# Three GpSimd multiplications moved behind a group of loads, and one output piece moved ahead of a tile's scores

## The chip, the core and the metric

The kernel runs on one core of a Trainium2 chip. The metric is the device time of one execution in microseconds (us), and the time given for the kernel before is the median of three runs.

## What is computed

A retention layer (an attention whose weights decay with distance) is followed by a feed-forward layer with a snake activation. Cut to what matters, the reference is:

```python
# q, k, v: 4 batches x 8 heads x 768 positions x 64
for t in range(768):
    state = gamma * state + outer(k[t], v[t])      # per batch and head
    y[t] = q[t] @ state / 8                        # 64 -> 1/sqrt(64)
x = y with heads side by side                      # 3072 tokens x 512
h = x @ w_in                                       # 512 -> 2048
g = h + sin(alpha * h)**2 / (alpha + 1e-9)
out = g @ w_out                                    # 2048 -> 512, float32
```

## The kernel before

**Tiles and groups.** The 768 positions of a batch are cut into 6 chunks of 128, so there are 24 tiles of 128 tokens by 512. `order` (P in the code) lists them: P[0] to P[3], also called e0 to e3, are the first chunks of the four batches, which need no state; then come chunks 1 to 5 of batch 0 (P[4] to P[8]), and so on. The sixth tile is P[5]. The tiles make groups: the first has four tiles, each of the other ten has two.

**One tile.** `stage_T` turns q and k on TensorE and copies them out of PSUM (DVE, line 279). `stage_A` makes the scores (PE, line 293) and multiplies them with the decay or the mask into `aT` (DVE, line 302). `stage_M` multiplies the state (line 332) and the scores (line 336) into the PSUM tile `py`, adds the tile to the state (line 312), and multiplies `py` with the decay table `qg[:, c]` of the tile's chunk into `xT` (DVE, line 343); then `keep_S` copies the state out (ScalarE, ACT in the profile, line 319). For a later chunk the next state needs v scaled by position: `scale_v` multiplies v in place by `kg` (line 155). `decay_table(c, engine)` makes `qg[:, c]` from `qg[:, 0]` (line 223).

**The feed-forward layer.** A `Slot(g, f)` is 128 hidden units of a group: 4 matmuls with w_in into a PSUM tile `ph` (line 567), the sine on ACT (line 570), the square on ACT (line 575) or on DVE (line 577, chosen with `sq("D")`), and the add on DVE (line 582), which reads the sine's square from SBUF and `ph` from PSUM, writes `gT` and frees `ph`. An output piece is one matmul of 128x512 with w_out (line 592); `F(ts, lo, hi)` issues pieces lo to hi-1 of token tile ts of the first group. The PSUM tiles with tag "mm" share four banks in turn; "ty", "pa" and "ps" are one bank each.

**The order of the work.** It is written out by hand, and each engine does its own instructions in the order of the program. For the first group that is lines 754 to 896, with the slots named w[0] to w[15], and w[20] and w[21] for the fourth tile's columns (four units each, 128 wide). In the order of the "mm" tiles there, w[7], w[6], w[3], w[5] are followed by w[20], w[21], w[11], w[9], and these by w[8], w[10], w[13], w[12].

**GpSimd's queue.** GpSimd (POOL in the profile) issues all loads of q, k, v and the weights, in the order of the program, and they go through one queue (q0). Lines 157 to 161 issue v of e0; q, k and v of e1 and of e2; w_in(0) and w_in(1) (quarters): nine loads. Lines 689 to 691 then run the three multiplications of the change, and lines 692 to 701 issue q, k, v of e3, the other six quarters of w_in and w_out, and q, k, v of P[4], P[5] and P[6]. Counted from the first, v of P[4] is the 21st load and q of P[5] the 22nd. Behind these stand more loads mixed with scalings of v (lines 779 to 810).

Of the kernel before, what the change touches and what calls it, by code (L numbers as in the profile page):

```python
# [15 lines left out]
def kernel(  # L16
# [15 lines left out]
    nc = tc.nc  # L32
# [36 lines left out]
    def chunk_of(t, j):  # L69
        b, c = divmod(j, NCH)  # L70
        return t[b, :, c * C:(c + 1) * C, :].rearrange("h s d -> s h d")

    def paired(j):

        return j in order[1:B]

    def pairs_of(t, j):
        b, c = divmod(j, NCH)
        return t[b, :, c * C:(c + 1) * C, :].rearrange("h (i f) d -> i h (f d)", f=2)

    def load_chunk(j, names="qkv"):
        for name, src in (("q", q), ("k", k), ("v", v)):
            if name not in names:
                continue
            if name == "v":
                t = big.tile([128, H, D], BF16, name="vr", tag="vr", bufs=10)
            elif name == "q" and paired(j):
                if "pairs" not in raw:
                    raw["pairs"] = work.tile([64, B, H, 2, D], BF16, name="qp", tag="gT", bufs=2)
                t = raw["pairs"][:, order.index(j)]  # L90
                nc.gpsimd.dma_start(out=t.rearrange("i h f d -> i h (f d)"), in_=pairs_of(src, j))
                raw[name, j] = t
                continue
            else:
                if ("qk", j) not in raw:
                    raw["qk", j] = big.tile([128, 2, H, D], BF16, name="qkr", tag="qkr", bufs=9)
                t = raw["qk", j][:, "qk".index(name)]
            nc.gpsimd.dma_start(out=t, in_=chunk_of(src, j))  # L98
            raw[name, j] = t
# [3 lines left out]
    def wide(j):  # L103
        return j >= NCH + 2 and j % NCH > 0
# [28 lines left out]
    def load_w_out(i):  # L133
        nc.gpsimd.dma_start(out=w_out[:, i * fo:(i + 1) * fo, :], in_=w_out_v[:, i * fo:(i + 1) * fo, :])
# [16 lines left out]
    def scale_v(j, eng):  # L151
        t, by = raw["v", j], kg
        if wide(j):
            t, by = t.rearrange("i f p d -> i (f p) d"), kgq
        eng.tensor_mul(t, t, by[:, j % NCH, :, None].to_broadcast([128, H, D]))  # L155
# [66 lines left out]
    def decay_table(c, eng):  # L222
        eng.tensor_mul(qg[:, c], qg[:, 0], step[:, c, :, None].to_broadcast([128, NP, C]))
# [43 lines left out]
    def stage_T(j, eng=None, tag="ty"):  # L267
        st["qkT", j] = work.tile([128, 2 * NP, 128], BF16, name="qkT", tag="qkT", bufs=6)
        copy = nc.scalar.copy if eng is nc.scalar else nc.vector.tensor_copy
        if paired(j):  # L270
            for i, t in enumerate((tag, "pa")):
                pt = psum.tile([128, NP, 128], BF16, name="pt", tag=t)
                turn_half(j, i, pt)
                leave_T(j, i, pt, copy)
            return
        pt = psum.tile([128, 2 * NP, 128], BF16, name="pt", tag=tag, bufs=4 if tag == "mm" else 1)
        for i in range(2):
            turn_half(j, i, pt[:, i * NP:(i + 1) * NP, :])
        copy(st["qkT", j], pt)
# [7 lines left out]
    def stage_A(j, parts=1):  # L287
        qkT = st["qkT", j]
        pa = psum.tile([128, 2, NP, 128], F32, name="pa", tag="pa")
        for p in range(NP):  # L290
            for e in range(2):
                r = slice(64 * e, 64 * e + 64)
                nc.tensor.matmul(pa[:, e, p, :], qkT[r, NP + p, :], qkT[r, p, :],  # L293
                                 start=(p == 0), stop=True, skip_group_check=True)
        aT = work.tile([128, 2, NP, 128], BF16, name="aT", tag="aT", bufs=2)
        flat = "p e n t -> p (e n) t"
        if parts > 1:
            for h in range(0, NP, NP // parts):
                r = slice(h, h + NP // parts)
                nc.vector.tensor_mul(aT[:, :, r], pa[:, :, r], dec[:, :, r])  # L300
        else:
            nc.vector.tensor_mul(aT.rearrange(flat), pa.rearrange(flat), dec.rearrange(flat) if j % NCH == 0 else mask_bc)  # L302
        st["aT", j] = aT
# [17 lines left out]
    def stage_M(j, tag="ty"):  # L321
        c = j % NCH
        g, i = place[j]
        if g not in xT:
            xT[g] = work.tile([128, KS, sizes[g] * C], BF16, name="xT", tag="xT", bufs=3)
        qkT, aT, vs = st["qkT", j], st["aT", j], raw["v", j]
        py = psum.tile([128, NP, 128], F32, name="py", tag=tag)
        if c > 0:
            for p in range(NP):
                for e in range(2):  # L330
                    r = slice(64 * e, 64 * e + 64)
                    nc.tensor.matmul(py[r, p, :], s_bd[c % 2][:, p, r], qkT[:, p, :],  # L332
                                     start=(p == 0), stop=True, skip_group_check=True)
        for p in range(NP):
            for e in range(2):
                nc.tensor.matmul(py[64 * e:64 * e + 64, p, :], vs[:, 2 * p + e, :], aT[:, e, p, :],  # L336
                                 start=(c == 0 and p == 0), stop=True, skip_group_check=True)
        x = xT[g][:, :, i * C:(i + 1) * C]
        if c == 0:
            nc.scalar.copy(x, py)  # L340
            return
        ps = stage_S(j) if c < NCH - 1 else None
        nc.vector.tensor_mul(x, py, qg[:, c])
        if ps is not None:
            if wide(j + 1):
                swapped(s_b[(c + 1) % 2][0], ps, nc.scalar.copy)
                swapped(s_f[0], ps, nc.vector.tensor_copy)
            else:
                keep_S(j, ps)
# [239 lines left out]
    def ff_out(g, ts, f):  # L589
        if (g, ts) not in po:  # L590
            po[g, ts] = psum.tile([128, d_model], F32, name="po", tag="mm", bufs=4)
        nc.tensor.matmul(po[g, ts], gT[g][:, f, ts * C:(ts + 1) * C], w_out[:, f, :],  # L592
                         start=(f == 0), stop=(f == FF - 1))
        if f == FF - 1:
            take(g, ts)
# [49 lines left out]
    e0, e1, e2, e3 = P[:B]  # L645
# [40 lines left out]
    nc.vector.reciprocal(rec_alpha, rec_alpha)  # L686
    decay_table(1, nc.vector)

    scale_v(e0, nc.gpsimd)
    decay_table(2, nc.gpsimd)  # L690
    decay_table(3, nc.gpsimd)
    load_chunk(e3)
    load_w_out(0)
    load_w_in(2)
# [2 lines left out]
    load_w_out(2)  # L697
    load_w_out(3)
    load_chunk(P[4])
    load_chunk(P[5])  # L700
    load_chunk(P[6])

# [44 lines left out]
    def F(ts, lo, hi):  # L747
        for f in range(lo, hi):
            ff_out(0, ts, f)
# [136 lines left out]
    SK(e0)()  # L886
    F(2, 6, 7)
    stage_T(P[5], nc.vector, "mm")
    F(2, 7, 10)
    scale_v(P[5], nc.vector)  # L890
    stage_A(P[5])
    F(2, 10, 11)
    stage_M(P[4])
    F(2, 11, 15)
    stage_M(P[5])
# [68 lines left out]
```

## Time and profile before

| what | value |
|---|---|
| median of three runs | 211.04 us (210.78 to 211.46) |
| the profiled execution | 210.3 us |
| its span, first to last instruction | 208.4 us |
| granted TensorE clock | 1.000 |
| PE busy | 202.9 us, 97% of the span |
| DVE, ACT busy | 158.7 and 159.5 us |
| GpSimd busy | 109.5 us, of which most stands before 125 us |
| the loads of q, k, v and weights (q0) | 13.38 MB in 75968 packets |

The profile comes from one execution; the times in it count from the start of its span. PE is TensorE, PEld its weight loads, DVE VectorE, ACT ScalarE, POOL GpSimd, SP the engine that issues the stores. A row of a timeline gives the start, the time from the first start to the last end, the engine, the line, the operation, the output and inputs, and how many instructions are merged; a bracket gives the idle time before the row and what ended it. The ends of matmuls are modelled, so rows of PE overlap a little.

### The profile page before, as it was taken

How to read it: one execution, taken by the hardware profiler on the slowest of the kernel's cores; microseconds unless marked ns; L12 is line 12 of the kernel's file. 1: busy time of each engine (PE TensorE's matmuls, PEld its weight loads, DVE VectorE, ACT ScalarE, POOL GpSimd, SP SyncE). 2: the span in 40 equal slices, each digit the busy share in tenths (PEclk: the TensorE clock that was granted, in tenths of full speed). 3: DMA queues.
4: the chain of work that ended last, by engine and by line, in shares of the span. 5: the costliest groups of instructions: out<-in, count | busy, mean ns of one | idle time of the engine just before them, and what ended most of it. 6: DMA issues, size and time to landing. Idle time of an engine off the chain costs nothing.

```text
span 208.4 us, 5987 instructions
## 1 busy us (share of the span) xinstructions
PE 202.9 (97%) x2427; PEld 132.3 (63%) x2427; DVE 158.7 (76%) x363; ACT 159.5 (77%) x344; POOL 109.5 (53%) x148
## 2 busy tenths in 40 slices
PE   6998999999999999999999999999999999999994
PEld 2654644567776667666666666666766766666653
DVE  7867897876988597787788778779878778686540
ACT  7858798548997878888888888886787787888821
POOL 8899333898979979999999330000413101000000
PEclk9999999999999999999999999999999999999999
DMA  8999999999999999999999903412415110110112
GB/s 128 156 199 179 201 207 179 155 211 183 132 115 96 193 178 162 170 139 176 174 142 174 173 36 68 101 46 58 104 53 55 53 50 3 53 50 0 50 53 101
DMA packets 98747, 24.78 MB, mean 119 GB/s; under 512 B 91280, under 2 KB 95776, under 8 KB 98720
## 3 DMA queue, kind: packets, MB, share of 16 engines
q0 software_dynamic: 75968, 13.38, 85.6%
q1 hardware_dynamic: 22608, 10.96, 25.0%
q8 instruction: 19, 0.31, 0.6%
q10 hardware_dynamic: 144, 0.07, 0.1%
q14 instruction: 8, 0.07, 0.1%
HBM read 27.27 MB, written 6.29 MB: 161 GB/s over the span
## 4 chain that ended last, share of the span: by engine, by line
PE 94%; DVE 3%; ACT 1%; issue 0%; DVEq 0%
PE ph L567 39%; PE po L592 39%; PE spare L637 3%; PE pa L293 2%; PE poh L617 2%; PE py L397 2%; PE pt L249 1%; PE py L336 1%; PE py L510 1%; PE py L332 1%; PE pa L413 1%; PE pa L433 1%; DVE gT L582 1%; PE ps L312 1%; DVE qkT L265 0%
## 5 line engine op out<-in xcount | busy, mean ns | idle before, releaser
L582 DVE SCALAR_TENSOR_TENSOR gT<-s,rec_alpha,ph 128x256 bf16<-128x256 f32 (+3 forms) x184 | 82.1, 489 | 26.6 <-ACT s L575 25.7
L570 ACT ACTIVATE s<-ph,alpha_sb 128x256 f32<-128x256 f32 (+3 forms) x184 | 79.1, 480 | 29.4 <-PE ph L567 28.3
L567 PE MATMUL ph<-xT,w_in 128*128 128x256 bf16 (+3 forms) x736 | 98.6, 277 | 0.0
L592 PE MATMUL po<-w_out,gT 128*128 128x512 bf16 x368 | 95.3, 380 | 0.0
L567 PEld LDWEIGHTS <-w_in 128*128 128x128 bf16 x736 | 70.5, 98 | 30.4 <-issue 0.4
L575 ACT ACTIVATE s<-s 128x512 f32<-128x512 f32 (+1 forms) x91 | 56.4, 623 | 2.7
L592 PEld LDWEIGHTS <-gT 128*128 128x128 bf16 x368 | 33.9, 98 | 25.9 <-DVE gT L582 0.3
L438 POOL CAST s_b<-s_f 128x256 bf16<-128x256 f32 x10 | 4.0, 399 | 45.4 <-DVE s_f L491 23.6
L121 POOL DMA_DIRECT2D qk_seq<-in_k_dram x24 | 17.1, 762 | 1.5 <-DMA qk_seq<-in_q_dram 1.5
L121 POOL DMA_DIRECT2D qk_seq<-in_q_dram x24 | 17.1, 750 | 1.3 <-issue 0.7
L604 DVE COPY o_sb<-po 128x512 f32<-128x512 f32 x19 | 13.1, 691 | 5.4 <-PE po L592 5.3
L121 POOL DMA_DIRECT2D v_seq<-in_v_dram x24 | 17.1, 785 | 0.0
L155 POOL TENSOR_TENSOR v_seq<-v_seq,kgq 128x512 bf16<-128x512 bf16 x14 | 14.8, 1101 | 4.2 <-DMA v_seq<-in_v_dram 4.2
L637 PE MATMUL spare<-warm 128*128 128x256 f32 (+3 forms) x22 | 10.1, 554 | 1.5 <-DVE warm L165 1.5
L98 POOL DMA_DIRECT2D vr<-in_v_dram x10 | 9.1, 913 | 3.9 <-DMA w_in<-in_moe_w_in_dram 2.0
L421 DVE TENSOR_TENSOR aTw<-pa,maskq 128x512 bf16<-128x512 f32 (+1 forms) x14 | 10.1, 723 | 0.2
L98 POOL DMA_DIRECT2D qkr<-in_k_dram x9 | 8.1, 899 | 3.3 <-DMA w_out<-in_moe_w_out_dram 3.2
L528 DVE TENSOR_TENSOR xT<-py,qg 128x256 bf16<-128x256 f32 x26 | 9.7, 417 | 0.0
L155 POOL TENSOR_TENSOR vr<-vr,kg 128x512 bf16<-128x512 bf16 x8 | 8.7, 1083 | 0.6 <-PE py L336 0.6
L577 DVE TENSOR_TENSOR s<-s 128x512 f32<-128x512 f32 (+1 forms) x7 | 4.4, 633 | 3.8 <-ACT s L570 3.8
L302 DVE TENSOR_TENSOR aT<-pa,mask 128x1024 bf16<-128x1024 f32 x6 | 7.3, 1219 | 0.0
L98 POOL DMA_DIRECT2D qkr<-in_q_dram x6 | 5.4, 896 | 3.6 <-DMA w_in<-in_moe_w_in_dram 2.1
(110 smaller groups left out, 153.0 us busy)
## 6 DMA issues: line engine op xcount, KB each, us to landing
out_dram<-o_sb SPq DMA_DIRECT2D x23, 256.0 KB, 3.0
w_in<-in_moe_w_in_dram POOLq DMA_DIRECT2D x4, 512.0 KB, 9.1
w_out<-in_moe_w_out_dram POOLq DMA_DIRECT2D x4, 512.0 KB, 13.0
vr<-in_v_dram POOLq DMA_DIRECT2D x10, 128.0 KB, 6.3
qk_seq<-in_q_dram POOLq DMA_DIRECT2D x16, 80.0 KB, 6.3
qk_seq<-in_k_dram POOLq DMA_DIRECT2D x16, 80.0 KB, 4.6
v_seq<-in_v_dram POOLq DMA_DIRECT2D x16, 80.0 KB, 3.8
qkr<-in_k_dram POOLq DMA_DIRECT2D x9, 128.0 KB, 7.1
```

Source lines behind the costliest of these rows:

```text
L98: nc.gpsimd.dma_start(out=t, in_=chunk_of(src, j))
L121: nc.gpsimd.dma_start(out=o, in_=src[bt, h, cs[0] * C:, :].rearrange("(f i) d -> i f d", i=64))
L155: eng.tensor_mul(t, t, by[:, j % NCH, :, None].to_broadcast([128, H, D]))
L421: nc.vector.tensor_mul(aT.rearrange("p e m t -> p e (m t)").rearrange("p e (n t) -> p e n t", t=t), pa[:, :, 0:2 * n].rearrange("p e (n t) ...
L528: nc.vector.tensor_mul(x[:, 2 * b:2 * b + 2, :], y.rearrange("p (m t) -> p m t", m=2), qg[:, c, 2 * b:2 * b + 2])
L567: nc.tensor.matmul(self.ph[:, m, :], w_in[:, i, f * 128:(f + 1) * 128], xT[g][:, i, self.lo:self.hi], start=(m == 0 and i == 0), stop=(i = ...
L570: nc.scalar.activation(out=self.s[:, m, :], in_=self.ph[:, m, :], func=ACTF.Sin, scale=alpha_sb[:, f:f + 1])
L575: nc.scalar.activation(out=self.s, in_=self.s, func=ACTF.Square)
L582: nc.vector.scalar_tensor_tensor(gT[self.g][:, f, self.lo:self.hi], self.s[:, m, :], rec_alpha[:, f:f + 1], self.ph[:, m, :], op0=ALU.mult ...
L592: nc.tensor.matmul(po[g, ts], gT[g][:, f, ts * C:(ts + 1) * C], w_out[:, f, :], start=(f == 0), stop=(f == FF - 1))
L604: nc.vector.tensor_copy(o_sb, po[g, ts])
L637: nc.tensor.matmul(spare["ps"][:, :m], warm[:, :128], warm[:, :m], start=True, stop=True)
```

## The change

Two edits in the written-out order; no instruction is added or left out.

1. `scale_v(e0)` and the decay tables 2 and 3, all on GpSimd, move from ahead of e3's loads to behind the loads of P[4], the fifth tile; twelve loads pass them.
2. The output piece 10 of token tile 2 moves from behind the sixth tile's scores (`stage_A(P[5])`) to ahead of its scaling and scores.

```diff
     decay_table(1, nc.vector)
 
-    scale_v(e0, nc.gpsimd)
-    decay_table(2, nc.gpsimd)
-    decay_table(3, nc.gpsimd)
     load_chunk(e3)
     load_w_out(0)
     load_w_in(2)
...
     load_w_out(2)
     load_w_out(3)
     load_chunk(P[4])
+    scale_v(e0, nc.gpsimd)
+    decay_table(2, nc.gpsimd)
+    decay_table(3, nc.gpsimd)
     load_chunk(P[5])
     load_chunk(P[6])
...
     stage_T(P[5], nc.vector, "mm")
-    F(2, 7, 10)
+    F(2, 7, 11)
     scale_v(P[5], nc.vector)
     stage_A(P[5])
-    F(2, 10, 11)
     stage_M(P[4])
     F(2, 11, 15)
     stage_M(P[5])
```

## The prediction

> **What bounds the kernel now.** I read the page first (busy shares, then the chain that ended last), then the clock by core (one core, granted clock 1.000), then each engine's timeline in the two stretches that the diff touches, the waits, and the issue-to-landing times of the loads.
>
> ```profile
> PE 202.9 (97%) x2427; PEld 132.3 (63%) x2427; DVE 158.7 (76%) x363; ACT 159.5 (77%) x344; POOL 109.5 (53%) x148
> ...
> PE 94%; DVE 3%; ACT 1%; issue 0%; DVEq 0%
> ```
>
> The end is set by TensorE (PE): 94% of the chain is PE work, and GpSimd (POOL) does not occur in it. So a change on GpSimd counts only where it makes PE wait, and whatever PE loses early is lost for good, since PE then runs to the end almost without a gap. The profiled execution took 210.3 us for a span of 208.4, so 1.9 lie around the span. The median of the runs is 211.04, that is 0.74 more; I work in the profiled execution and add 0.74 at the end. A difference under 0.3% (0.63 us) is about what a measurement of this kernel cannot tell from no change.
>
> **Part one, GpSimd's queue.** This is GpSimd's own timeline, in the order start, duration, line; the bracket is the idle time before and what ended it.
>
> ```profile
> 9.42 1.04 POOL L155 TENSOR_TENSOR vr<-vr,kg 128x512 bf16<-128x512 bf16 x1 [0.58 <-PE py L336]
> 10.43 2.03 POOL L223 TENSOR_TENSOR qg<-qg,step 128x512 f32<-128x512 f32 x2
> 12.41 0.75 POOL L91 DMA_DIRECT2D qp<-in_q_dram  x1
> ...
> 22.44 0.88 POOL L98 DMA_DIRECT2D vr<-in_v_dram  x1 [1.31 <-DMA w_out<-in_moe_w_out_dram]
> 25.39 0.88 POOL L98 DMA_DIRECT2D qkr<-in_q_dram  x1 [2.07 <-DMA w_in<-in_moe_w_in_dram]
> 27.81 0.87 POOL L98 DMA_DIRECT2D qkr<-in_k_dram  x1 [1.54 <-DMA w_out<-in_moe_w_out_dram]
> ```
>
> *What goes.* At 9.42 to 12.41 GpSimd runs three multiplications, 2.99 us with starts 1.01, 0.99 and 0.99 apart, after waiting 0.58 for PE. Without them the loads of e3 can be issued from 8.84, 3.57 us sooner. That buys nothing, because the transfers are what is full. The stretches from 9 to 15 us moved 155, 169, 193, 202, 210 and 216 GB/s with no gap. The two quarters of w_in issued at 7.28 and 8.06 landed 7.4 and 9.2 us later, at 14.7 and 17.2, and e3's q, k and v right behind them at 18.1, 18.7 and 19.5, then w_out(0) at 22.2. The loads go through one queue (q0) in the same order as before, so their landings stay. The issues soon catch on the other limit too: the 21st load (v of P[4], 22.44) was released by the landing of the 13th (w_out(0)), the 22nd by that of the 14th, the 23rd by that of the 15th. Eight are in flight at most, so the 16th now waits for the 8th (14.7), the 17th for the 9th (17.2), and the 21st still goes at 22.44. I price this at 0.
>
> *What it delays.* The three multiplications come behind the 21st load: 22.44 + 0.89 (the spacing of such a load to the multiplication behind it, 44.06 to 44.95) = 23.33, and end at about 26.32. The 22nd load (q of P[5]) then goes at 26.3 instead of 25.39, the 23rd at 27.81 as before. This is free: the 22nd landed only 13.6 us after its issue, because four quarters of w_in and w_out (about 2.5 us each: w_out(0) to w_out(3) land at 22.2, 27.5, 32.7, 35.3 with w_in's between) and P[4]'s three loads stood ahead of it. The results have time: the scaled v of e0 is read at 40.70 (L312), the tables by P[5]'s and P[6]'s products at 45.65 and 53.16. At 0 again. If that cover were gone, P[5]'s transposes at 40.96 have 1.1 us of margin (k lands at 39.9).
>
> *What it collides with.* Here I find the price. DVE's timeline in the new place:
>
> ```profile
> 23.25 0.55 DVE L577 TENSOR_TENSOR s<-s 128x384 f32<-128x384 f32 x1
> 23.72 1.66 DVE L582 SCALAR_TENSOR_TENSOR gT<-s,rec_alpha,ph 128x384 bf16<-128x384 f32 x3
> 26.06 0.69 DVE L577 TENSOR_TENSOR s<-s 128x512 f32<-128x512 f32 x1 [0.69 <-ACT s L570]
> 26.79 1.12 DVE L582 SCALAR_TENSOR_TENSOR gT<-s,rec_alpha,ph 128x128 bf16<-128x128 f32 x4
> 27.83 0.69 DVE L577 TENSOR_TENSOR s<-s 128x512 f32<-128x512 f32 x1
> 28.55 3.10 DVE L582 SCALAR_TENSOR_TENSOR gT<-s,rec_alpha,ph 128x128 bf16<-128x128 f32 x7
> ```
>
> The squares of line 577 read both operands from SBUF; the adds of line 582 read one tensor from SBUF and one from PSUM. In the old place (9.4 to 12.4) DVE runs only instructions with one operand in PSUM. In the new place w[3]'s square starts at 23.25, a hair before 23.33, and w[20]'s is ready at 26.06, inside the last table (25.33 to 26.32). No row of this trace has a GpSimd multiplication beside a DVE instruction with two SBUF tensors. The nearest rows are GpSimd's multiplication beside one-tensor adds (52.28: 1.05 us, the adds 0.445 each) and GpSimd's DMA issues beside a two-tensor DVE multiplication (42.33 and 43.20: 0.88, 0.89), neither slowed. So the lower end is 0, and a gain is excluded because DVE's instructions in the old place last as long as elsewhere (L302 1.22 at 9.64, 1.23 at 21.06). The upper end is that the second to start waits for the whole of the first.
>
> Worked out at that end: the scaling waits for the square (23.80), so GpSimd's three run 23.80 to 26.80; w[20]'s square, ready at 26.06, waits until then, 0.75 late. Behind it DVE is busy without a pause until 31.65, so w[20]'s and w[21]'s adds are 0.75 late, and PE needs the PSUM banks they free. The line that shows that PE has no slack there is the weight load of w[10]:
>
> ```profile
> 29.73 0.53 PEld L567 LDWEIGHTS <-w_in 128*128 128x128 bf16 x3 [0.16 <-issue]
> ```
>
> w[21]'s four adds end at 28.55 + 4 x 0.28 = 29.67, and w[10] starts at 29.73 in the fourth bank after w[21]: the margin is 0.05. So PE starts w[10] at 30.47, **+0.75**. Should the scaling start first, the square waits from 23.25 to 24.37, w[6]'s add (the first of the three from 23.72, 0.55 each, so ending at 24.3) ends near 25.4, and w[21], which takes its bank, starts there instead of at 24.7 (after 16 of the 32 matmuls that start at 23.80 and last 1.79): about +0.75 as well. I take this end, as likelier than not by a little: each near row lacks one of the two conditions, and nothing behind the square absorbs a delay. That is a judgement, and I keep 0 in the range.
>
> [...]
>
> **Part two, the output piece.** PE, then DVE, around the sixth tile's scores:
>
> ```profile
> 41.62 0.81 PE L592 MATMUL po<-w_out,gT 128*128 128x512 bf16 x3
> 42.57 0.40 PE L293 MATMUL pa<-qkT 64*128 64x128 bf16 x8
> 42.90 0.39 PE L592 MATMUL po<-w_out,gT 128*128 128x512 bf16 x1
> 43.22 0.41 PE L332 MATMUL py<-qkT,s_bd 128*64 128x128 bf16 x8
> ...
> 43.92 1.04 PE L592 MATMUL po<-w_out,gT 128*128 128x512 bf16 x4
> 44.90 0.41 PE L332 MATMUL py<-qkT,s_bd 128*64 128x128 bf16 x8
> ```
> ```profile
> 43.03 1.22 DVE L302 TENSOR_TENSOR aT<-pa,mask 128x1024 bf16<-128x1024 f32 x1
> 44.16 0.68 DVE L343 TENSOR_TENSOR xT<-py,qg 128x512 bf16<-128x512 f32 x1
> ```
>
> Three pieces of 0.217 end at 42.27 and PE waits for DVE's copy (41.83 + 0.70) until 42.57. A fourth fills that wait: 41.62 + 4 x 0.217 + 0.1 for the change of shape = 42.59. The piece at 42.90 goes, so P[4]'s mix starts at 42.9 instead of 43.22, 0.32 sooner, and the four pieces end at about 44.57. But P[5]'s mix writes the PSUM bank "ty" that P[4]'s product of line 343 reads until 44.16 + 0.68 = 44.84, and that product follows DVE's copy, scaling and mask (41.83, 42.43, 43.03), which do not move. So PE starts P[5]'s mix at 44.89 as before: the stall moves from 42.3 to 44.6. Priced at 0, from +0.02 to -0.3 if the bank is not what is late.
>
> **Sum:** 0 + 0 + 0.75 + 0 = +0.75; 210.3 becomes 211.05, and the median 211.8.
>
> **Rivals.**
> 1. *The two engines do not hold each other up* (the end that is not slower). Place: the squares at 23.25 and 26.06; it decides if either is delayed by less than PE's 0.05 of slack at w[10] or the 0.35 at w[21]. For it: both near rows. Against: neither row is the pair. Time: 211.0.
> 2. *Faster.* P[5]'s mix does not wait for the bank, so 0.32 stays won, and the sooner issues bring w_in(1) early enough to end the 0.32 that PE's weight load waited for it at 17.21: 0.64, 210.4. Against: the order of the queue and the product at 44.84.
> 3. *The delayed loads become late.* The 22nd load is issued 0.9 to 1.4 late; if the queue ran dry it and those behind it would land so, P[5]'s k at 41.3 against 40.96, and the later tiles behind them: +0.4 to +0.7, on top of the 0.75 at worst: 211.4 to 212.5. Against: v of P[4], which stands ahead in the queue, lands only at 38.1, so the queue has 11 us of work when the 22nd is issued.
>
> **Chances.** Forecast 0.50 (211.5 to 212.3; 0.42 of it beyond 0.3%, 0.08 within), rival 1 0.27 (within), rival 2 0.16 (0.13 beyond, 0.03 within), rival 3 0.07 (beyond). So slower 0.49, same 0.38, faster 0.13. The range 210.4 to 212.4 takes in both ends of the collision and most of rival 2.
>
> **What would show it.** GpSimd's three multiplications at 23.3 to 26.8 with the first longer than 1.04 or late; a square of line 577 longer than 0.55 or 0.69, or starting late with the releaser named as POOL or "issue"; w[8] and w[10] on PE later by half a microsecond or more; everything from 31 us on shifted by the same amount. Squares at 0.55 and 0.69 on time mean rival 1. In part two, P[4]'s mix 0.3 sooner but P[5]'s not. e3's q landing before 18.1 would break the claim that the queue was full, and a PE wait on a load near 41 would mean rival 3.

## The result, and the profile after

The changed kernel takes 213.73 us (median of 6 runs, 213.51 to 214.7), the kernel before 211.12 beside it (6 runs, 210.78 to 211.83). The ratio is 1.0129 with a 95% interval of 1.0102 to 1.0156: **2.6 us slower**. The forecast was 211.8 in a range up to 212.4, so the sign was right and the size was not.

The profiled execution of the changed kernel took 213.8 us for a span of 212.0, at a granted clock of 1.000. Against the profiled execution of before that is 3.5 us, 0.9 more than the medians differ; the execution of before was a quick one of its kind. From the page of the changed kernel, the busy shares, the chain that ended last, and the group of DVE's squares (busy time, mean ns, idle time before), and last the same group in the kernel before:

```profile
PE 203.5 (96%) x2427; PEld 132.7 (63%) x2427; DVE 163.0 (77%) x363; ACT 160.0 (75%) x344; POOL 109.6 (52%) x148
...
PE 92%; DVE 6%; ACT 1%; issue 0%
...
L577 DVE TENSOR_TENSOR s<-s 128x512 f32<-128x512 f32 (+1 forms) x7 | 7.6, 1088 | 3.1 <-ACT s L570 3.1
```
```profile
L577 DVE TENSOR_TENSOR s<-s 128x512 f32<-128x512 f32 (+1 forms) x7 | 4.4, 633 | 3.8 <-ACT s L570 3.8
```

PE still sets the end, but DVE's share of the chain doubled from 3% to 6%, and DVE is busy 4.3 us longer with the same 363 instructions. Of these 4.3, 3.2 lie in one group: seven squares took 7.6 us where they took 4.4 before. Now the new place, GpSimd's and DVE's timelines of the changed kernel (start, duration, engine, line):

```profile
22.97 0.88 POOL L98 DMA_DIRECT2D vr<-in_v_dram  x1 [1.55 <-PE ph L567]
23.86 1.06 POOL L155 TENSOR_TENSOR vr<-vr,kg 128x512 bf16<-128x512 bf16 x1
24.87 2.04 POOL L223 TENSOR_TENSOR qg<-qg,step 128x512 f32<-128x512 f32 x2
...
45.16 1.08 POOL L155 TENSOR_TENSOR vr<-vr,kg 128x512 bf16<-128x512 bf16 x1
```
```profile
23.58 3.75 DVE L577 TENSOR_TENSOR s<-s 128x384 f32<-128x384 f32 x1
27.26 1.65 DVE L582 SCALAR_TENSOR_TENSOR gT<-s,rec_alpha,ph 128x384 bf16<-128x384 f32 x3
...
45.61 1.20 DVE L155 TENSOR_TENSOR vr<-vr,kg 128x512 bf16<-128x512 bf16 x1
```

w[3]'s square lasts 3.75 instead of 0.55. It **started first** (23.58, GpSimd's scaling at 23.86), and it ends at 27.33, which is 0.42 behind the end of the third multiplication (24.87 + 2.04 = 26.91). GpSimd's three are as long as in the old place (1.06 and 2.04, against 1.04 and 2.03). At 45.6 there is a second, smaller meeting: DVE's scaling of P[5]'s v, 0.68 before, takes 1.20 beside GpSimd's scaling of P[6]'s v. There GpSimd started first, and DVE's scaling ends at 46.81, 0.57 behind the end of GpSimd's (46.24). What PE makes of it, and ahead of it the row of the kernel before for w[20] and w[21]:

```profile
23.80 1.95 PE L567 MATMUL ph<-xT,w_in 128*128 128x128 bf16 x32
```
```profile
24.12 1.06 PE L567 MATMUL ph<-xT,w_in 128*128 128x128 bf16 x16
27.91 1.05 PE L567 MATMUL ph<-xT,w_in 128*128 128x128 bf16 x16 [2.73 <-DVE gT L582]
...
48.59 0.41 PE L332 MATMUL py<-qkT,s_bd 128*64 128x128 bf16 x8 [0.77 <-DVE xT L343]
```

Before, PE ran w[20]'s and w[21]'s 32 matmuls in one piece. Now it waits 2.73 us between them for a PSUM bank that DVE's adds, queued behind the square, free late. Landmarks of the two profiled executions:

| landmark on PE | before | after | later by |
|---|---|---|---|
| first w_in matmul (L567) | 15.17 | 15.49 | 0.32 |
| w[20] and w[21] | 23.80 | 24.12 | 0.32 |
| w[10] (L567) | 29.73 | 32.90 | 3.17 |
| P[5]'s mix (L332) | 44.90 | 48.59 | 3.69 |
| from there to the end of the span | 163.50 | 163.41 | |

The first 0.32 is there before any instruction of the change matters to PE (its transposes at 6.16 come at 6.48, and GpSimd's queue differs only from 8.75 on), and is taken as a difference between executions. The square costs 3.17 - 0.32 = **2.85**, the second meeting 3.69 - 3.17 = **0.52**, and behind the 49th microsecond nothing is won or lost.

### The profile page after: what moved, and what is told of

Read it like the earlier page. It is cut to its first block, busy times and chain, and to the rows that moved or that the text cites. A ratio compares the mean times of both kernels' runs of the same rounds, so it can differ in the third digit from the quotient of the medians.

```text
span 212.0 us, 5987 instructions
## 1 busy us (share of the span) xinstructions
PE 203.5 (96%) x2427; PEld 132.7 (63%) x2427; DVE 163.0 (77%) x363; ACT 160.0 (75%) x344; POOL 109.6 (52%) x148
## 4 chain that ended last, share of the span: by engine, by line
PE 92%; DVE 6%; ACT 1%; issue 0%
PE ph L567 38%; PE po L592 37%; PE spare L637 5%; DVE s L577 2%; PE poh L617 2%; PE py L397 2%; PE pa L293 2%; PE pt L249 1%; DVE gT L582 1%; DVE aT L302 1%; PE py L510 1%; PE pa L413 1%; PE py L336 1%; PE py L332 1%; PE pa L433 1%; DVE vr L155 1%
## 5 line engine op out<-in xcount | busy, mean ns | idle before, releaser
L567 PE MATMUL ph<-xT,w_in 128*128 128x256 bf16 (+3 forms) x736 | 98.8, 277 | 2.9 <-DVE gT L582 2.7
L567 PEld LDWEIGHTS <-w_in 128*128 128x128 bf16 x736 | 70.6, 98 | 33.4 <-issue 3.0
L637 PE MATMUL spare<-warm 128*128 128x256 f32 (+3 forms) x22 | 10.6, 575 | 1.5 <-DVE warm L165 1.5
L577 DVE TENSOR_TENSOR s<-s 128x512 f32<-128x512 f32 (+1 forms) x7 | 7.6, 1088 | 3.1 <-ACT s L570 3.1
L319 ACT CAST s_bd<-ps 64x256 bf16<-64x256 f32 x12 | 4.4, 363 | 3.6 <-PE ps L312 3.5
```

The costliest lines, as they stand in the source:

```text
L567: nc.tensor.matmul(self.ph[:, m, :], w_in[:, i, f * 128:(f + 1) * 128], xT[g][:, i, self.lo:self.hi], start=(m == 0 and i == 0), stop=(i = ...
L577: nc.vector.tensor_mul(self.s, self.s, self.s)
L637: nc.tensor.matmul(spare["ps"][:, :m], warm[:, :128], warm[:, :m], start=True, stop=True)
```

## The experiments

Two theories went into the first batch. **The run holds:** a DVE instruction with two SBUF tensors is held until all of GpSimd's multiplications in a row are done. **The rival:** it is held for one of them only (the sum on record), and the rest comes from elsewhere, the queue, the piece or the bank. Diffs are against the kernel before unless another is named. Times are medians, with the kernel before run on the same chip.

### e1: the queue's edit alone

```diff
-    scale_v(e0, nc.gpsimd)
-    decay_table(2, nc.gpsimd)
-    decay_table(3, nc.gpsimd)
     load_chunk(e3)
...
     load_chunk(P[4])
+    scale_v(e0, nc.gpsimd)
+    decay_table(2, nc.gpsimd)
+    decay_table(3, nc.gpsimd)
```

> Only the three GpSimd multiplications are moved; the output piece stays where it was. Theory (GpSimd's multiplications starve a DVE multiplication of two SBUF tensors for as long as they follow one another): the square of w[3] lasts about 3.7 us instead of 0.55, PE starts w[21] about 2.8 later, a later collision of GpSimd's scaling at 45.2 with DVE's scaling of P[5] may add 0.5; 213.5 to 214, the time of the whole change. Rival A (the loads that are issued sooner or later make the loss): the same total, but PE waits on loads. Rival B (the piece in part two has a share): at least 0.4 less than the whole change.

Measured: 215.06 us (4 runs, 214.45 to 215.87) against 211.05, ratio 1.0169 (1.0128 to 1.0211). So the queue's edit alone makes the loss, here even more than the whole change made in the first measurement. The PE timeline of e1 and one stretch of its table by windows (window, length, busy times of PE, PEld, DVE, ACT and POOL, granted clock, DMA share, GB/s):

```profile
28.75 1.05 PE L567 MATMUL ph<-xT,w_in 128*128 128x128 bf16 x16 [2.94 <-DVE gT L582]
...
30.00 3.43 PE L567 MATMUL ph<-xT,w_in 128*128 128x512 bf16 x8
```
```profile
30.00:32.00 2.00, 2.00 (x6) 0.76 (x5) 1.96 (x6) 1.03 (x5) 0.54 (x1) 0.50 1.24 205
```

The square, 24.20 to 28.16, started 0.5 ahead of GpSimd's recorded start and was again held to the end of the run (27.74 + 0.42). New is what comes behind PE's wait: eight matmuls that take 1.89 us in the changed kernel take 3.43 here, at a granted clock of 0.50. That is another 1.5 us, and with the output piece ahead of them, 0.57 instead of 0.38, some 1.7. The mean granted clock of all four runs of e1 is 0.991 or 0.992, where the six of the changed kernel show 1.000 or 0.999.

### e9 and e10: the change and its first part again, on one chip

e9 is the changed kernel, e10 is e1. The question was whether the piece of part two saves PE's clock.

> The changed kernel as it is, on one chip with the next. Theory (the hold, then PE's wait; the clock falls only after a PE wait somewhat longer than 2.73 us): the square of w[3] lasts 3.6 to 4.0 us; where PE's wait stays near 2.7 the clock stays at 1.000 and the time is 213.4 to 214, where it reaches 2.9 the clock falls to half for some 3.5 us and the time is 215. Rival (the piece of part two keeps the clock up): the clock stays at 1.000 however long the wait.

> The three GpSimd multiplications moved, the output piece not, on one chip with the changed kernel. Theory: the same wait of PE for w[6]'s add as the changed kernel on this chip, and the same clock; within 0.5 us of it. Rival (the piece has a share): over 1 us slower than the changed kernel on the same chip, with a clock near 0.992.

Measured: e9 215.31 us (4 runs, 214.68 to 215.72), ratio 1.0201 (1.0166 to 1.0236); e10 214.26 (4 runs, 212.95 to 215.22), ratio 1.0149 (1.0098 to 1.0201). e10 is not slower than e9; its median is even 1.05 lower, more than the 0.5 expected, though the intervals overlap. So nothing here gives the piece a share in the clock. The clock fell in one of four runs of either kernel, while it fell in all four of e1, which is the same kernel as e10: 0.991 in e10's profiled run (PE waits 2.96 at w[21], then 0.52 in the stretch from 30 to 32 us), 0.992 in one run of e9, and 1.000 in e9's profiled run (the wait is 2.86).

e9's interval lies above that of the first measurement of the same kernel. e9's time was expected at 213.4 to 214 as long as the clock stays up, and it came out above that. Its profiled execution shows where 1.1 of it are. The stretch from P[5]'s mix (48.76) to the end is 164.5 us long instead of 163.4, and holds a third meeting, on DVE and on GpSimd:

```profile
52.67 2.40 DVE L577 TENSOR_TENSOR s<-s 128x512 f32<-128x512 f32 x1 [1.65 <-ACT s L570]
```
```profile
52.77 1.05 POOL L155 TENSOR_TENSOR vr<-vr,kg 128x512 bf16<-128x512 bf16 x1
53.76 1.40 POOL L121 DMA_DIRECT2D qk_seq<-in_k_dram  x2
```

That square is 0.69 long in the changed kernel's first profile, where GpSimd's scaling starts at 53.98, 0.8 behind the square's end. PE then waits 0.94 for the add behind it. So the total depends on which of GpSimd's scalings DVE's squares happen to meet, and this differs from run to run. That this accounts for all runs of e9 is inferred from its one profile.

### e4 and e5: the scaling alone, the tables alone

e4 moves only `scale_v(e0, nc.gpsimd)`, e5 only the two lines of `decay_table`.

> The kernel before with the scaling of e0's v alone behind the loads of P[4]; the two tables stay in the old place. One GpSimd instruction of 1.05 us collides. Theory (starving, as long as GpSimd's run): the square of w[3] lasts about 1.6 to 1.7 us, PE starts w[21] about 0.8 late, 211.7 to 212.1. Rival (a fixed price of a collision, whatever the length of the run): 2.8 more, 214.

> The kernel before with the two tables alone behind the loads of P[4]; the scaling stays in the old place. Two GpSimd instructions of 1.0 us each, back to back. Theory (starving through the gap between them): the square lasts about 2.6 us, PE starts w[21] about 1.7 late, 212.6 to 213.1. Rival (the square gets in between two GpSimd instructions): about 1.6 us, 0.8 more, 211.9.

e5 took 212.71 us, ratio 1.0072 (1.0044 to 1.01). Its DVE, then its GpSimd:

```profile
23.43 2.78 DVE L577 TENSOR_TENSOR s<-s 128x384 f32<-128x384 f32 x1
```
```profile
23.73 2.05 POOL L223 TENSOR_TENSOR qg<-qg,step 128x512 f32<-128x512 f32 x2
```

The square ends at 26.21, 0.43 behind GpSimd's run of two (25.78): one multiplication less in the run, a hold shorter by one multiplication (2.78 against 3.75). e4 took 211.74, ratio 1.0017 (0.9991 to 1.0043). It does not answer its question: in its profile the loads came late, GpSimd issued P[4]'s v at 24.52 and scaled at 25.42, and the square (24.45 to 25.00) was done by then. That its median lies in the expected range is chance. What a single scaling costs in this place stays unmeasured.

### e3: w[3]'s square on ACT

Against the changed kernel:

```diff
-    w[3].sq("D")
+    w[3].sq("A")
```

> The changed kernel with the square of w[3] on ScalarE instead of DVE, so that the first collision has no two-tensor DVE instruction; the loads are as in the changed kernel. Theory: no wait of PE for w[6]'s add; the square of w[20], ready at about 26, meets the last GpSimd table and is held for 0.4 to 0.9, so 211.5 to 212.1. Rival (the loads make the loss): 213.7 as the changed kernel.

Measured: 211.35 us, ratio 1.0006 (0.9981 to 1.003). With the one instruction gone from DVE that meets the run, the whole loss is gone, though GpSimd's order and the loads are those of the changed kernel. w[20]'s square met the last table and took 1.01 instead of 0.69. PE does show that: from the output pieces behind w[9] to w[10] it takes 2.52 us (28.82 to 31.34) where the kernel before takes 2.21 (27.52 to 29.73). These 0.31 are lost in the noise of the total, but they bear out the path of the sum on record, in which a late square of w[20] makes w[10] late by as much.

### e6 and e7: multiplications and memsets added to the kernel before

In the kernel before, with its three multiplications in the old place, e6 adds work without use behind P[4]'s loads, and e7 four memsets of the same tile.

```diff
     load_chunk(P[4])
+    for n in range(3):
+        nc.gpsimd.tensor_mul(warm, warm, warm)     # e6
+    for n in range(4):
+        nc.gpsimd.memset(warm, 0.0)                # e7
```

> The kernel before, unmoved, with three more GpSimd multiplications (128x512 float32, a scratch tile with itself, nothing reads the result) behind the loads of P[4]; about 3 us of GpSimd. Theory (starving): the square of w[3] is stretched to about 3.6 us and the time goes up by 2.4 to 2.9 though no load is issued sooner, 213.5 to 214. Rival A (the loads issued sooner make the loss): no stretch, 211.1. Rival B (the second to start waits for one instruction of the other, as forecast): 0.7 to 0.8 more, 211.9.

> The kernel before, unmoved, with four GpSimd memsets of 128x512 float32 on a scratch tile behind the loads of P[4]: GpSimd writes SBUF and reads no tensor. Theory (the hold is on reading): the square of w[3] keeps its 0.55 us, 211.1 within 0.3. Rival (any GpSimd instruction on SBUF holds it): the square is stretched over the memsets, 1 to 3 us more.

e6 took 211.82 us, ratio 1.0038 (1.0013 to 1.0063). Here **the theory failed and the rival was right**. DVE and GpSimd of e6:

```profile
24.35 1.89 DVE L577 TENSOR_TENSOR s<-s 128x384 f32<-128x384 f32 x1
...
27.74 1.06 DVE L577 TENSOR_TENSOR s<-s 128x512 f32<-128x512 f32 x1
```
```profile
24.76 3.50 POOL L701 TENSOR_TENSOR warm<-warm 128x512 f32<-128x512 f32 x3
```

Three multiplications run from 24.76 to 28.26 (one by one: 24.76, 25.90 and 27.22), but the square ends at 26.24, 0.42 behind the end of the first (24.76 + 1.06 = 25.82). The difference to the change: each of these reads what the one ahead wrote, so the program makes it wait for it. That gave the second question, whether it is the wait between them that lets DVE in. e7 took 211.09, ratio 0.9989 (0.9966 to 1.0011), but its square (24.00 to 24.55) was over before the memsets began (24.74), so it says nothing; memsets come again in e11.

### e11 and e13: the meeting by itself

Both have their test behind the last tile, where PE is done, so their totals mean nothing (225.7 and 224.4 us of span, one run each) and their rows are read. DVE runs multiplications of 128x384 with two SBUF tensors back to back; GpSimd is released into the middle of them.

```diff
+    series(0)                                     # 5 DVE multiplications each
+    series(1)
+    for f in range(3):                            # e11, row 1: independent, no DMA ahead
+        nc.gpsimd.tensor_mul(w_out[:, f, :]..., qg[:, 1], qg[:, 2])
...
+    nc.gpsimd.dma_start(out=w_out[:, 8, :]..., in_=chunk_of(v, 0))    # e13, row 1: DMA, then independent
+    for f in range(3):
+        wide_mul(f, qg[:, 1])
...
+    nc.gpsimd.dma_start(out=w_out[:, 9, :]..., in_=chunk_of(v, 0))    # e13, row 2: DMA, then dependent
+    wide_mul(3, qg[:, 1])
+    for f in (4, 5):
+        wide_mul(f, w_out[:, f - 1, :]...)
```

> The kernel before with a test behind its last tile, on memory that is no longer used, so its total time says nothing: DVE multiplies two SBUF tensors (128x384) in rows of ten, and beside the first row GpSimd runs three multiplications back to back, beside the second a DMA issue and one multiplication right behind it, beside a last row of five four memsets. Theory (a run of GpSimd multiplications holds DVE to its end): in the first row one DVE instruction lasts 3.0 to 3.6 us, the others 0.45 to 0.55. Rival (they take turns): several of 1 to 1.5 us. [...] In the last, if only GpSimd's reading holds DVE, all five stay below 0.6.

> The kernel before with another test behind its last tile (its total time says nothing): DVE multiplies two SBUF tensors (128x384) in rows of ten; beside the first row GpSimd issues a DMA and then runs three multiplications that do not depend on each other; beside the second it issues a DMA and runs three of which each reads the result of the last, so that each waits for all of the one ahead. [...] Rival (turns always): no DVE instruction over 2.5 us in either row.

e11, row 1, was against the theory: three independent multiplications with no DMA ahead did not hold DVE. The two engines **took turns**. DVE's three were 1.62, 1.61 and 1.61 long (0.55 alone), GpSimd's 1.43, 1.57 and 1.57 (the same multiplication takes 1.26 to 1.28 under the hold of e13). Row 2 of e11 put one DMA issue ahead of one multiplication: DVE was held from 215.78 for 2.37, that is from within the DMA issue (215.47 to 216.42), 0.66 ahead of GpSimd's recorded start (216.44), to 0.43 behind its end. Row 3: beside four memsets DVE's four take 0.54 each, so GpSimd's writes alone do not hold it.

e13 put the two together, DMA and run. DVE, then GpSimd, in its row 1:

```profile
206.85 4.81 DVE L939 TENSOR_TENSOR w_in<-qg 128x384 bf16<-128x384 f32 x1
```
```profile
206.55 0.96 POOL L948 DMA_DIRECT2D w_out<-in_v_dram  x1 [32.18 <-DVE w_out L945]
207.53 3.71 POOL L943 TENSOR_TENSOR w_out<-qg 128x512 bf16<-128x512 f32 x3
```

One DVE multiplication of 0.55 us lasts 4.81. It starts 0.30 into the DMA issue and 0.68 ahead of GpSimd's recorded start, and ends (211.66) 0.42 behind the end of the run (211.24). In row 2, with each multiplication waiting for the one ahead, DVE's three are 2.34, 1.51 and 1.51 long: held for the first, then turns. The rival, turns always and at most 2.5 us in either row, is refuted by the 4.81; the hold is longer than the 3.75 of the changed kernel because each of these three multiplications takes some 1.27, where the three there took 3.05 from first start to last end (23.86 to 26.91). So the two conditions of the loss are told apart: **a DMA issue directly ahead, and a run without a wait in it**.

For a *single* GpSimd multiplication behind a DMA issue this does not settle what happens. e11's row 2 was held to its end. But in five meetings of the kernels with one scaling of v behind a DMA issue (two in e1, one each in e5, e10 and e12), a DVE instruction that started within the issue was let go 0.90 ahead of the scaling's end: it took 1.00 to 1.45 us instead of 0.68 or 0.69, and the scaling 1.27 to 1.48 instead of 1.05 to 1.08. In e10, for example, DVE first, then GpSimd:

```profile
44.50 1.35 DVE L155 TENSOR_TENSOR vr<-vr,kg 128x512 bf16<-128x512 bf16 x1
```
```profile
45.28 1.46 POOL L155 TENSOR_TENSOR vr<-vr,kg 128x512 bf16<-128x512 bf16 x1
```

### e15: the same change with a small dependent pair ahead of the run

Against the changed kernel, ahead of the run of three that held w[3]'s square, two instructions of one element in each partition, the second of which waits for the first:

```diff
     load_chunk(P[4])
+    nc.gpsimd.memset(tiny, 0.0)
+    nc.gpsimd.tensor_mul(tiny, tiny, tiny)
     scale_v(e0, nc.gpsimd)
```

> [...] Rival (any run of three holds DVE): the square lasts over 3 us, 213.5 to 215.5.

Measured: 211.53 us (10 runs, 210.95 to 213.45), ratio 1.003 (0.9997 to 1.0063). One of the ten, 213.45, is as slow as the changed kernel, and it has no profile. GpSimd and DVE of e15:

```profile
23.48 0.19 POOL L698 TENSOR_TENSOR tiny<-tiny 128x1 f32<-128x1 f32 x1
23.62 1.04 POOL L155 TENSOR_TENSOR vr<-vr,kg 128x512 bf16<-128x512 bf16 x1
24.63 2.34 POOL L223 TENSOR_TENSOR qg<-qg,step 128x512 f32<-128x512 f32 x2
```
```profile
24.12 0.95 DVE L577 TENSOR_TENSOR s<-s 128x384 f32<-128x384 f32 x1
```

The same three multiplications in the same place, and the square gets its turn behind the first (25.07, 0.41 behind 24.66): it takes 0.95, not over 3 as the rival has it, though more than the 0.55 that it takes alone. It came later against the run than in the changed kernel, 0.50 into the scaling, so this profile alone would also fit a hold for one instruction; with e13's rows 1 and 2 it does not need that. PE's wait at w[21] is gone, and of a loss of 2.6 to 4.3 us some 0.6 is left in the median. The pair takes the DMA issue away from directly ahead and puts a wait there, both at once, so e15 does not tell the two conditions apart.

### e2 and e8: the piece alone, and the piece with another bank

e2 is the second edit of the change by itself. e8 adds to it that P[5]'s mix gets one of the four "mm" banks:

```diff
-        py = psum.tile([128, NP, 128], F32, name="py", tag=tag)
+        py = psum.tile([128, NP, 128], F32, name="py", tag=tag, bufs=4 if tag == "mm" else 1)
...
-    stage_M(P[5])
+    stage_M(P[5], "mm")
```

> Only the output piece is moved. Theory (part two only moves a stall, because the sixth tile's mix waits for the PSUM bank that DVE's product of the fifth frees): 0 within 0.1, the mix of P[4] 0.3 sooner, that of P[5] at 44.9 as before, with DVE L343 as the releaser. Rival (the bank is not what is late): 0.3 us faster.

> The output piece is moved, and the sixth tile's mix writes one of the four shared PSUM banks instead of the bank that the fifth tile's product still reads. Theory (the bank is what is late): the mix of P[5] starts 0.3 sooner than in the kernel before, about 44.6, and the whole is 0.2 to 0.35 us faster, 210.8. Rival (ACT's copy of the state or DVE's mask is late next): at most 0.1 faster.

e2 took 211.61 us (12 runs), ratio 1.0013 (0.9989 to 1.0038): no change. e8 took 211.38, ratio 0.9993 (0.9967 to 1.0018). P[5]'s mix on PE, first in e2, then in e8; in both the pieces ahead of it start at 45.53:

```profile
46.60 0.41 PE L332 MATMUL py<-qkT,s_bd 128*64 128x128 bf16 x8 [0.26 <-DVE xT L343]
```
```profile
46.27 0.41 PE L332 MATMUL py<-qkT,s_bd 128*64 128x128 bf16 x8
```

The wait for DVE's read of the bank is gone in e8, and the mix starts 0.33 sooner, as the piece had promised. The total, forecast to fall by 0.2 to 0.35 us, shows nothing outside its interval of about 0.5 to either side.

e2 also showed what the one profile of before had not. It has GpSimd's old order, and its queue ran thin: 124 GB/s from 17 to 20 us, where the profile of before has 183, and PE waited 0.60 for w_out(0).

### e12, e14 and e16: the new order without the first meeting

e12 and e16 are one kernel: the changed one with w[3]'s and w[20]'s squares on ACT and P[5]'s mix in an "mm" bank. e14 is that with the three multiplications back in the old place.

```diff
-    w[3].sq("D")
+    w[3].sq("A")
...
-    w[20].sq("D")
+    w[20].sq("A")
...
-    stage_M(P[5])
+    stage_M(P[5], "mm")
```

> The changed kernel with the squares of w[3] and w[20] on ScalarE, so that no two-tensor DVE instruction meets the three GpSimd multiplications, and P[5]'s mix in one of the shared banks. Theory (all the loss is the hold): 210.7 to 211.3, level with the kernel before. Rival (the sooner loads cost something, or are worth something): over 0.5 away on either side.

> As e12 (both squares on ScalarE, the piece moved, the mix in a shared bank), but with the three GpSimd multiplications in the old place, ahead of e3's loads. Theory (the sooner loads are worth something in most executions: PE waited 0.5 to 0.7 us for w_out(0) in e2, e7 and e8): 0.3 to 0.6 slower than e16 on the same chip, with a wait of PE for w_out. Rival (the sooner loads are worth nothing, as forecast): within 0.2 of e16.

> e12 as it is, on one chip with e14. Theory: 0.3 to 0.6 faster than e14 and than the kernel before, 210.4 to 210.8. Rival: level with e14.

| kernel | median us (runs) | ratio to the kernel before | 95% interval |
|---|---|---|---|
| e12, new order | 210.56 (10) | 0.9975 | 0.9958 to 0.9992 |
| e16, the same again | 210.64 (12) | 0.9978 | 0.9954 to 1.0002 |
| e14, old order | 210.96 (12) | 0.9994 | 0.9967 to 1.002 |

DVE's scaling of P[5]'s v still meets GpSimd in e12's profile (43.14, 1.45 instead of 0.68). With the bank of its own P[5]'s mix no longer waits for it, but the mask behind the scaling is late (44.52 to 45.73), and PE's product with the scores (L336) starts 0.50 behind the mix instead of 0.25 as in e16, where the two do not meet. Without the first meeting, the version with the new order is 0.4 us faster than the kernel before in e12; in e16 the interval just touches 1. The sooner loads would be worth the 0.32 between e14 and e16, but the intervals overlap, and e14's profile shows no wait of PE for w_out(0) that they would have ended. Their worth is not settled.

## Why the prediction was right in sign and wrong in size

- **What bounds the kernel: right.** What PE lost by 49 us stayed lost; the rest is 163.50 and 163.41.
- **What it collides with: the right place, and the step that failed.** "The upper end is that the second to start waits for the whole of the first" made one multiplication the most that could be lost, and let the order of the starts decide. No run shows the term of 0.75; in its place 2.85 was measured, because w[3]'s square, though first to start, was held through all three multiplications. The sum let that square pass and made w[20]'s the late one; in the run w[20]'s square came behind the whole run and took 0.68. What happened is the path that the prediction has for the other order: w[3]'s square late, w[6]'s add behind it, the bank, w[21] late, and from there w[10], with no slack. The 3.20 of the hold less the 0.35 of slack at w[21] are the 2.85. e5 (two multiplications, 2.78), e11's row 1 (no DMA issue ahead, turns) and e13 (a DMA issue and three, 4.81, and turns as soon as there are waits between) show what decides for a run of two or three: a DMA issue directly ahead, and no wait in the run.
- **The order of the starts: wrong.** The pair of instructions was the right one: with w[3]'s square on ACT the loss is gone (e3, 211.35 us), and beside GpSimd's memsets, which read no tensor, DVE's multiplications kept their 0.54 (e11). The order was not: the square started 0.28 ahead of GpSimd's recorded start here, 0.5 in e1, DVE's multiplication 0.68 in e13, and DVE lost each time. Where GpSimd's recorded start came first, at 45.16 here, at 26.77 in e3 and at 45.33 in e9, DVE did wait for the end of that one instruction, and took 1.20, 1.01 and 1.13 us instead of 0.68 or 0.69. The holds in e11 and e13 began within the DMA issue, 0.66 and 0.68 ahead of the multiplication's recorded start; why a DVE instruction that starts first is held, no row shows.
- **A second meeting, missing from the sum.** DVE and PE came 3.2 us late to the 45th microsecond and GpSimd's queue did not: its scaling of P[6]'s v stands at 45.16 (44.95 before), and DVE's scaling of P[5]'s v, 42.43 before, came at 45.61. That cost 0.52 more. A delay had been treated as a shift of everything behind it; it is one only for engines that wait for the delayed one.
- **What goes, priced at 0: not refuted, but read from one quick execution.** The signs on record held: e3's q, issued at 8.75 instead of 12.41, landed at 18.6, not sooner than 18.1, and the 16th, 17th and 21st load were issued at 15.47, 18.00 and 22.97, behind the landings of the 8th, 9th and 13th (15.2, 17.7 and 22.7). But "the transfers are what is full" holds for the profile of before (183 GB/s from 17 to 20 us) and not for e2's of the same order (124, and a PE wait of 0.60). e12 leaves room for a few tenths.
- **What it delays, at 0: right.** The stage from 32.90 on shows no wait of PE for a load near 41 us.
- **Part two, at 0: right, and for the reason given.** In the changed kernel P[4]'s mix stands at 46.09, 2.87 later than before where all around it is 3.17 later, so 0.30 was won there, and P[5]'s mix did not keep it. e2 measured no change, and e8 took the bank away and found the 0.33 in its profile.
- **The rivals.** Without blocking (211.0) is refuted by the square, faster (210.4) and late loads by the landmarks; the second quarter of w_in, which was to come sooner, landed at 17.7 instead of 17.2. The range left the time out because its upper end for the collision was the wait for one instruction, where the nearest rows bounded nothing; three multiplications in a row, 2.99 us, were in the profile and could have been the upper end.

## What to carry to other kernels

Before a GpSimd tensor instruction is moved, list the DVE instructions in the new place that read two SBUF tensors (one of 0.55 us became 3.75 here), and take as the upper end the whole run of GpSimd instructions up to the next wait, above all where a DMA issue stands directly ahead (4.81 in e13, turns of 1.61 and 1.62 without the issue in e11); a square on ACT (e3, 211.35 us) or a small dependent pair of GpSimd instructions ahead of the run (e15, 211.53) took most of the loss away here. A delay on one engine did not shift the others (with PE 3.2 late, GpSimd's scaling of P[6]'s v stood at 45.16, 44.95 before), so look again for new meetings behind it. Look at more than one execution before a queue is called full (183 and 124 GB/s from 17 to 20 us in two of the same order).

## What the runs showed of the hardware that was not expected

- **A DVE instruction held for a run of GpSimd's:** 0.55 became 3.75, 3.96, 3.88 and 3.98 (the changed kernel, e1, e9, e10) and 4.81 us (e13); each hold ended 0.42 to 0.43 behind the end of GpSimd's run.
- **Turns where GpSimd has no DMA issue directly ahead (e11) or waits between its multiplications (e13):** DVE 1.5 to 1.6 instead of 0.55, and GpSimd 1.35 to 1.57 where the same form takes some 1.27 under the hold; a table of e15 takes 1.34 instead of 1.04 behind the square's turn. So GpSimd is slowed there too. Under the hold it was not slowed in the kernel (1.06, and 2.04 for two); the three in e13's row 1 took 3.71.
- **A hold into DMA issues:** e9's square at 52.67 ended at 55.07, 1.25 behind the end of the only multiplication beside it (53.82) and just ahead of the next (55.16), with two DMA issues between. Why it was let go there stays open.
- **A clock that falls behind a wait.** After PE waits of 2.94 (e1) and 2.96 (e10) the granted clock was 0.50 for some 3.4 us (in windows of half a microsecond), at 1.7 us of loss (from w[21] to the next three output pieces 4.5 us instead of 2.8); after 2.73 and 2.86 it stayed at 1.00. It fell only 0.4 to 1.0 us after PE was at work again (28.5 against 28.08 in e10, some 29.7 against 28.75 in e1). Four profiles do not fix the edge.
